# An attention and GLU block on one core: column tiles for the GLU, a finer second chunk, more exponentials on VectorE

## The chip, the cores and the metric

The kernel runs on one core of a Trainium2 chip. The metric is the device time of one execution in microseconds (us). The core has TensorE (PE in the profile; PEld are its weight loads), VectorE (DVE), ScalarE (ACT), GpSimd (POOL) and SyncE (SP), which issues the DMAs. The granted TensorE clock of the profiled execution was 0.998 of full speed.

## The reference, cut to what matters

```python
B, S, D, H, Df = 1, 2048, 640, 32, 1728              # head width 20
x = A_x                                              # bf16, as all weights
n = layernorm(x)
q, k, v = heads(n @ wqkv)                            # (3, H, S, 20)
p = softmax(einsum("bhqd,bhkd->bhqk", q, k) * 20**-0.5)
h = x + merge(einsum("bhqk,bhkd->bhqd", p, v)) @ wo
m = layernorm(h)
out = h + (gelu(m @ w_gate) * (m @ w_up)) @ w_down   # tanh form of gelu
```

The scores are 32 heads of 2048 x 2048 values. Every one of these 134 million values needs an exponential.

## The kernel before, in words

**A planner orders everything.** The kernel does not write instructions in order. Each piece of work is registered with `op` (L58): its engine, a modelled duration, a priority (lower is sooner), what it reads and writes, and the PSUM banks that it takes (`acq`) and gives back (`rel`). `Sched.schedule` (L91) then plays all engines through time and picks, for each engine when it is free, the ready operation of the best priority. The result is a fixed order for each engine's queue, and `emit` (L239) writes it out with semaphore waits. Every instruction goes through one line of `emit`, so L359 of the profile stands for many kinds of work; there the tile names tell them apart. A `Bank` object lists the PSUM banks (0 to 7) that a piece of work may use. The planner knows three array shapes of PE: "row" (weights of 32 rows, four row groups), "col" (weights of at most 32 columns, four column groups) and "full" (128 by 128). For operations of priority 1 and up it prefers the shape that PE is in, since a change has a modelled cost of 0.098 us. When PE would be idle for long it inserts matmuls without use ("warm").

**Chunks, slots and tiles.** The 2048 queries are cut into chunks (`SIZES`, L310): 512, 512, 256, 256, 256, 128, 128. The 32 heads form 8 groups of four heads. A slot is 512 columns of work: one group for a chunk of 512, two groups for 256, four for 128. There are 32 slots in all. Each slot has 64 score tiles of 128 keys by 512 columns: 16 for each of the four heads of a group. A head's 20 values of q and k lie in one of four row groups of 32 rows, so tiles of different heads (index j) can be multiplied at the same time.

**Scores and exponentials.** `unit` (L895) takes two or three tiles in turn: the score matmuls (L919, shape "row") go to PSUM banks 0 to 2 or 3 to 4, and one ScalarE instruction makes the exponentials of all of them (`pts`, or a spare part in `rege`). Some tiles do not go to ScalarE. A quad is the four heads' tiles of one place, and `D_QUADS` (L326) sets how many quads of each slot go to VectorE: none in the first slot, then 3, 3, 3, 2, 2, 2, 1 by chunk, 79 in all. Such a tile ("d tile") is scored behind one of the units, into bank 7 or 5. VectorE scales it into 16-bit integers (L840, four of these for a quad). Then it forms four different terms from all 2048 columns, and each term is multiplied with V; their sum stands in for the exponential. A quad on VectorE so has four PV steps instead of one. Which of the four tiles goes behind which unit is chosen from the quad that comes next, a head not in the unit if there is one.

**PV and the sums.** `pv_op` (L855) multiplies the exponentials with V (21 columns of weights, the last one of ones, so that the row sums come out as well) in shape "col", four heads in four column groups, and adds up in bank 6. `epilogue` (L984) copies a slot's result to `osb`. For all chunks but the last `spread` (L969) sends the sums through DRAM (`sums`, then `rc`), VectorE takes the reciprocals, and they go through DRAM again (`rsums`) to be broadcast into `bsum`. GpSimd multiplies (`on16`), and the result goes to DRAM (`attn`). The last chunk takes a shorter way with PE transposes.

**After a chunk.** `post` (L1040) is registered when the last slot of a chunk is done: load the attention result, out projection (`chain`, L640, 160 matmuls of 320 columns in all), add x, layer norm, transposes, then gate and up (`mms`, L1095: 28 blocks of 128 weights by five steps), gelu, product, and down (L1159, 448 matmuls of 320 columns). These use banks 7 and 5, low priorities, and shape "full". For the first chunk ScalarE computes Gelu itself, which needs another activation table. For later chunks `gelu` (L1028) uses tanh, which lies in the table of the exponentials, and five VectorE instructions around it, with a temporary buffer in the part of `qt_all` that held the second block of 512 queries. The buffers `h_sb`, `hnT` and `ha` hold 512 tokens; a chunk of 256 takes one half (`base`, L963).

**Before the slots** come the layer norm of x and the projections of q, k and v, which run on into the first slots.

Of the kernel before, what the change touches and what calls it, by code (L numbers as in the profile page):

```python
# [16 lines left out]
SEM_ANY = 0.036  # L17
# [4 lines left out]
PE_AGE = 1.5  # L22

# [3 lines left out]
class Bank:  # L27

    __slots__ = ("allowed", "b")

    def __init__(self, *allowed):
        self.allowed = allowed
        self.b = None
# [5 lines left out]
class Op:  # L39
    __slots__ = ("i", "eng", "fns", "dur", "lat", "prio", "deps", "succ", "nd", "ready",  # L40
                 "acq", "rel", "sem", "tag", "mode", "start", "fin", "pos", "know", "util")


class Sched:
# [13 lines left out]
    def op(self, eng, fns, dur, prio, reads=(), writes=(), acq=(), rel=(), after=(), sem=None, lat=None, mode=None, util=0.0):  # L58
        if eng == "dve" and rel and prio > self.ev:
            prio = self.ev  # L60
        o = Op()
        o.i = len(self.ops)
        o.eng, o.dur, o.lat, o.sem = eng, dur, DRAIN[eng] if lat is None else lat, sem
        o.util = util
        o.mode = mode
        o.tag = writes[0] if writes else None
        o.fns = fns if isinstance(fns, list) else [fns]
        o.prio = (prio, o.i)
        deps = set(after)
        for r in reads:  # L70
            if r in self.lw:
                deps.add(self.lw[r])
        for w in writes:
            if w in self.lw:
                deps.add(self.lw[w])
            deps.update(self.rd.get(w, ()))
        for r in reads:
            self.rd.setdefault(r, []).append(o.i)
        for w in writes:
            self.lw[w] = o.i  # L80
            self.rd[w] = []
        deps.discard(o.i)
        o.deps = deps
        o.acq = list(acq)
        o.rel = list(rel)
        o.succ = []
        o.ready = 0.0
        self.ops.append(o)
        return o.i

    def schedule(self):  # L91
# [19 lines left out]
        recent = collections.deque()  # L111
        live = False
        due = None
        total = len(ops)
        while done < total:
# [4 lines left out]
            for e in ENGINES:  # L120
# [8 lines left out]
                while ready[e]:  # L129
# [10 lines left out]
                    for bk in o.acq:  # L140
                        for b in bk.allowed:
                            if owner[b] is None and free_at[b] <= t + 1e-9 and b not in got and b not in kept:
                                got.append(b)
                                break
                        else:
                            got = None
                            break
                    if got is None:

                        if p[0] == 0:  # L150
                            kept.update(bk.allowed[0] for bk in o.acq)
                        skipped.append((p, i))
                        continue
# [20 lines left out]
                if chosen is None:  # L174
                    if e == "pe" and self.warm is not None:
# [4 lines left out]
                        if sum(x for _, x in recent) < WARM_MIN * WARM_WIN and (free7 or live):  # L180
                            o = Op()
                            o.i, o.eng, o.lat = len(ops), "pe", DRAIN["pe"]
                            o.prio, o.sem, o.tag, o.util = (9, 0), None, "warm", 0.213
                            o.acq, o.rel, o.succ, o.dur = [], [], [], 0.215
                            if live and (mode[e] == "col" or not free7):
                                o.fns, o.mode, o.deps = list(self.pad), "col", set()
                            else:
                                b = fb[0]
                                o.fns, o.mode = [self.warm[b]], "full"
                                o.deps = set(self.warm_deps) | ({last[b]} if last[b] is not None else set())  # L190
                                last[b] = o.i
# [6 lines left out]
                if e == "pe" and self.pad is not None and o.tag and o.tag[0] == "O":  # L198
# [10 lines left out]
                o.start = t  # L209
                if e == "act":  # L210
                    due = t + o.dur + (0.905 if o.dur > 1.2 else 1.332) - QK_LEAD if o.mode == "exp" else None
# [9 lines left out]
                for bk in o.rel:  # L221
                    b = bk.b
                    owner[b] = None
                    free_at[b] = o.fin + SEM_LAT.get((e, "pe"), SEM_ANY)
# [85 lines left out]
SIZES = (512, 512, 256, 256, 256, 128, 128)  # L310
# [15 lines left out]
D_QUADS = (3, 3, 3, 2, 2, 2, 1)  # L326
D_QUADS0 = 0
SIX = ()
D_FIRST, D_SPAN = 0, 18
GELU_A = 2.0 * 0.7978845608028654  # L330
# [4 lines left out]
P_QK, P_PV, P_PRO, P_EPI, P_LN, P_BG = 0, 1, 1.5, 2, 2.5, 3  # L335


def bass_sequential_preLN__mha_block__glu_gated_geglu__prompt_kernel(
# [12 lines left out]
    with ExitStack() as es:  # L351
# [42 lines left out]
        rc = sb("rc", [128, 2, 16], FP32)  # L394
        bsum = sb("bsum", [128, 512], FP32)
# [242 lines left out]
        def chain(bk, key, n, steps, reads, prio, acq=True, after=()):  # L638
            for k, (l, r) in enumerate(steps):
                yield op("pe", lambda eng, l=l, r=r, k=k: eng.matmul(  # L640
                    bank(bk, n), l, r, start=(k == 0), stop=(k == len(steps) - 1)),
                    c_mm(n), prio, mode="full", util=n / 2400.0, reads=reads, writes=[key], acq=[bk] if (k == 0 and acq) else [],
                    after=after if k == 0 else ())
# [148 lines left out]
        for s_, (c, gs) in enumerate(slots):  # L792
            mine = list(dict.fromkeys(x[1:3] for x in tiles if x[0] == s_))
            n = D_QUADS[c] if s_ else D_QUADS0
# [5 lines left out]
        while rem:  # L800
# [9 lines left out]
            if k[1] < want:  # L810
                n -= six
                q = d_rem[s_]
                js = [x[3] for x in rem[0:n]]
                near = [x for x in q if x[1:3] == q[0][1:3]]
                xd = min(near, key=lambda x: x[3] in js)
                q.remove(xd)
# [7 lines left out]
        assert not any(d_rem.values())  # L824
        pv_slot, pv_n, pv_ops = [0], [0], []
        pv_start = {}
        pv_wait, d_wait = [], []
        last_qk = {c: [] for c in range(len(CHUNKS))}
# [5 lines left out]
        def d_exp(b, tile, prio):  # L834
            c = slots[tile[0]][0]
            e = min(c, 2)
            h = len(d_raw)
            v, vk = d_v[e][d_n[e] % len(d_v[e])]
            aft = tuple(e_ops) + (tuple(last_qk[0]) if c else ()) + (tuple(last_qk[1]) if c > 1 else ())
# [55 lines left out]
        def unit(u):  # L895
# [39 lines left out]
            qk = op("pe", fns, 0.215, P_QK, mode="row", util=0.0533 * len(al), reads=reads, writes=[("S", u), "qkseq"] + ([("SD", xd)] if six else []), acq=bks)  # L935
            for x in al:
                last_qk[slots[x[0]][0]].append(qk)
            if six:
                bd = bks[2]
            elif xd:  # L940
                bd = Bank(*BG[slots[xd[0]][0]])
                qd = op("pe", [qk_mms(lambda: bank(bd), xd, kk) for kk in range(512 // CHUNKS[slots[xd[0]][0]][1])], 0.08,
                        P_QK + 0.5, mode="row", util=0.0533, reads=qk_reads(xd), writes=[("SD", xd)], acq=[bd], after=[qk])
                last_qk[slots[xd[0]][0]].append(qd)
# [18 lines left out]
        def base(c):  # L963
            n = CHUNKS[c][1]
            if n == 128:
                return 2 + (c == len(CHUNKS) - 1)
            return 2 * (c % 2) if n < 512 else 0

        def spread(s, c, gs, nq):  # L969
            n = len(gs)  # L970
            h = lambda dst, src, reads, key, sem, issue: dma(dst, src, key, reads, sem + str(s), 3.2, P_EPI, issue, keep=False)
            h(sdr[s], osb[DH:128:32, s, :], [("osb", s)], ("sdr", s), "sa", 0.1)
            h(rc[:, s, :], sdr[s].rearrange("j (a b) -> (j a) b", b=16), [("sdr", s)], ("rc", s), "sb", 0.4)
            op("dve", I("reciprocal", rc[:, s, :], rc[:, s, :]), 0.25, P_EPI, reads=[("rc", s)], writes=[("rc", s)])
# [9 lines left out]
        def epilogue(s_, bk):  # L984
# [9 lines left out]
            b2 = Bank(*BG[c])  # L994
# [6 lines left out]
            for tt in range(4):  # L1001
                op("pe", lambda eng, tt=tt: eng.transpose(bank(b2)[:, tt * 128:(tt + 1) * 128],
                                                          osb[:, s, tt * 128:(tt + 1) * 128], identf[:]),
                   c_mm(128, 2.5), P_EPI, mode="full", reads=[("osb", s), "identf"], writes=[key], acq=[b2] if tt == 0 else [],
# [3 lines left out]
            op("dve", lambda eng: eng.reciprocal(rcv, bv()[:, :, :, DH]), 0.17, min(P_EPI, sc.ev), reads=[key], writes=[("rc", s)])  # L1008
            for gi, g in enumerate(gs):
# [4 lines left out]
                   c_dve(80 * nt), min(P_EPI, sc.ev), reads=[key, ("rc", s)], writes=[("on", g, tb + tt) for tt in range(nt)],  # L1014
# [25 lines left out]
        def post(c, banks, tail):  # L1040
            p = P_EPI if tail else P_LN
# [10 lines left out]
            for tt in range(tb, tb + nt):  # L1052
                t = q0 // 128 + tt - tb
                i = t % 2
                if tail:
                    transposes(o_nat[:, 0, :], [("on", g, 0) for g in range(NG)], oT[:, :, tt * 128:(tt + 1) * 128],
                               ("hnT", tt), banks, P_EPI, "act", after=first)
                for hf in range(2):
                    bk = Bank(*banks)
                    key = ("bk", sc_id())  # L1060
                    list(chain(bk, key, 320, [(oT[:, a, tt * 128:(tt + 1) * 128], wo[:, a, hf * 320:(hf + 1) * 320])
                                              for a in range(NA)], [("hnT", tt), "wo"], p, after=(sc.lw[("h", tt, hf)],)))
# [26 lines left out]
            def mms(k, w, wkey, after):  # L1089
                bk, key = Bank(*banks), ("bk", sc_id())  # L1090
                for fi in range(min(fn_, NF - k * fn_)):
                    f = k * fn_ + fi
                    for a in range(NA):
                        st = fi == 0 and a == 0
                        op("pe", lambda eng, a=a, f=f, fi=fi: eng.matmul(  # L1095
                            bank(bk)[:, fi * nq:(fi + 1) * nq], w[:, a, F0[f]:F0[f] + 128], hnT[:, a, 128 * tb:128 * tb + nq],
                            start=(a == 0), stop=(a == NA - 1)),
                           c_mm(nq), p, mode="full", util=nq / 2400.0, reads=hk + [(wkey, 0)], writes=[key], acq=[bk] if st else [],
# [24 lines left out]
            else:  # L1123

                cp, gl = [], []
                for k in range(nb):
# [3 lines left out]
                    if c:  # L1130
# [8 lines left out]
                for ks in [] if c else [list(range(i, min(i + 4, nb))) for i in range(0, nb, 4)]:  # L1139
# [11 lines left out]
            for tt in range(tb, tb + nt):  # L1151
                t = q0 // 128 + tt - tb
                i = t % 2
                for hf in range(2):
                    bk = Bank(*banks)
                    key = ("bk", sc_id())
                    for f in range(NF):
                        o = hb + f * nq + (tt - tb) * 128
                        op("pe", lambda eng, f=f, o=o, hf=hf, bk=bk: eng.matmul(  # L1159
                            bank(bk, 320), ha_f[:, o:o + 128], wd[:, f, hf * 320:(hf + 1) * 320],  # L1160
                            start=(f == 0), stop=(f == NF - 1)), c_mm(320), p, mode="full", util=0.133, reads=hkeys(f // fn_) + [("wd", 0), "wd2", "wdz"],
# [15 lines left out]
                        skip_group_check=True) for b in sc.warm_banks}  # L1177
        sc.pad = [I("matmul", PS[32 * j:32 * j + 32, 512 * 6:512 * 7], zer[:], kt_all[:, 0, 0:512], start=False, stop=False,
                    tile_position=(0, 32 * j), skip_group_check=True) for j in range(4)]
        sc.warm_deps = tuple(sc.lw[kk] for kk in k_keys[0][0])  # L1180
        for kt in range(NT):
            proj_v(kt, 0, (6, 7), P_EPI if kt < 4 else P_BG, "dve")
        
        ui = 0
        for s_, (c, gs) in enumerate(slots):
            if c == 0:
                g = s_
                if g + 1 in STEP:
                    t, (g0, g1) = g + 1, STEP[g + 1]
                    pr = P_EPI if t == 1 else P_BG  # L1190
# [3 lines left out]
                if g < 3:  # L1194
                    for kt in range(NT * g // 3, NT * (g + 1) // 3):
# [60 lines left out]
```

## Time and profile before

| | us |
|---|---|
| median of 3 runs | 899.21 (899.01 to 900.5) |
| the profiled execution | 899.9 |
| its span | 898.2 |
| first exponential starts, last one ends | 35.6, 858.9 |
| busy: PE, ACT, DVE, POOL | 836.4, 851.0, 689.6, 75.0 |
| exponentials on ScalarE: 346 of 1536 columns, mean; 347 of 1024 columns, mean | 1.50, 1.07 |
| d tile evictions on VectorE: 316, mean | 0.687 |
| reciprocals of the sums on VectorE: 30, mean | 0.243 |

How to read it: busy time of PE holds waits, since matmuls are pipelined and their ends are modelled. An instruction's duration overlaps that of the one behind it on its engine, by 0.08 us or so, so that 15 tiles on ScalarE take 6.78 us though the six durations add up to more. In a row of a group, the number behind x is the count, then come busy time and the mean duration, then the idle time of the engine before them.

### The profile page before, as it was taken

How to read it: one execution, taken by the hardware profiler on the slowest of the kernel's cores; microseconds unless marked ns; L12 is line 12 of the kernel's file. 1: busy time of each engine (PE TensorE's matmuls, PEld its weight loads, DVE VectorE, ACT ScalarE, POOL GpSimd, SP SyncE). 2: the span in 40 equal slices, each digit the busy share in tenths (PEclk: the TensorE clock that was granted, in tenths of full speed). 3: DMA queues.
4: the chain of work that ended last, by engine and by line, in shares of the span. 5: the costliest groups of instructions: out<-in, count | busy, mean ns of one | idle time of the engine just before them, and what ended most of it. 6: DMA issues, size and time to landing. Idle time of an engine off the chain costs nothing.

```text
span 898.2 us, 24425 instructions
## 1 busy us (share of the span) xinstructions
PE 836.4 (93%) x10745; PEld 359.1 (40%) x10809; DVE 689.6 (77%) x1263; ACT 851.0 (95%) x777; POOL 75.0 (8%) x147
## 2 busy tenths in 40 slices
PE   3999999899989899999999899999999999999988
PEld 2532222222223222323344333334445446666657
DVE  7839888888989888787778889965669669658553
ACT  6699999999999999999999999999999999999960
POOL 5000000000001100000000100000102000020100
PEclk9999999999999999999999999999999999999999
DMA  7211120222244510000111110011111010031000
GB/s 264 84 50 49 32 67 29 64 81 66 73 137 135 152 46 17 17 14 5 39 51 54 33 34 17 18 30 48 29 54 33 18 48 18 20 63 26 10 17 15
DMA packets 55937, 46.17 MB, mean 51 GB/s; under 512 B 25492, under 2 KB 49392, under 8 KB 55832
## 3 DMA queue, kind: packets, MB, share of 16 engines
q1 hardware_dynamic: 55832, 44.62, 17.8%
q8 instruction: 84, 1.38, 0.6%
q14 instruction: 21, 0.17, 0.1%
HBM read 30.68 MB, written 11.04 MB: 46 GB/s over the span
## 4 chain that ended last, share of the span: by engine, by line
ACT 46%; PE 46%; DVE 6%; issue 1%; DMA 1%; DVEq 0%
ACT pts L359 35%; PE ps L919 14%; PE ps L359 11%; ACT rege L359 10%; PE ps L1095 9%; PE ps L640 6%; PE ps L1159 5%; DVE rege L359 1%; DVE qt_all L359 1%; DVE rege L840 1%; ACT qt_all L359 1%; DVE stats L359 1%; DVE rege L1131 1%; PE ps L585 1%; DMA rege<-xn_t 1%
## 5 line engine op out<-in xcount | busy, mean ns | idle before, releaser
L359 ACT ACTIVATE pts<-ps 128x1536 bf16<-128x1536 f32 x578 | 652.6, 1242 | 10.2 <-PE ps L919 5.7
L919 PE MATMUL ps<-qt_all,kt_all 32*128 32x256 bf16 (+2 forms) x3584 | 320.8, 288 | 25.7 <-ACT pts L359 16.7
L919 PEld LDWEIGHTS ps<-qt_all,kt_all 32*128 32x128 bf16 x3584 | 103.3, 92 | 236.0 <-ACT pts L359 128.3
L840 DVE TENSOR_SCALAR rege<-ps 128x512 int16<-128x512 f32 x200 | 137.0, 687 | 58.6 <-PE ps L919 56.4
L359 ACT ACTIVATE rege<-ps 128x1536 bf16<-128x1536 f32 x115 | 172.1, 1496 | 1.5 <-PE ps L359 0.7
L1095 PE MATMUL ps<-rege,regw 128*128 128x256 bf16 (+2 forms) x951 | 151.6, 289 | 8.4 <-DVE rege L359 2.9
L359 PE MATMUL ps<-pts,v_all 128*21 128x256 bf16 (+2 forms) x2472 | 134.0, 287 | 0.0
L359 PE MATMUL ps<-rege,v_all 128*21 128x512 bf16 (+2 forms) x1564 | 127.6, 312 | 1.3 <-DVE rege L359 1.0
L840 DVE TENSOR_SCALAR qt_all<-ps 128x512 int16<-128x512 f32 x116 | 79.8, 688 | 42.5 <-PE ps L919 40.9
L1095 PEld LDWEIGHTS ps<-rege,regw 128*128 128x128 bf16 x980 | 74.2, 99 | 65.7 <-issue 31.5
L359 POOL TENSOR_TENSOR on<-osb,bsum 128x512 bf16<-128x512 f32 x30 | 42.0, 1399 | 648.2 <-DMA bsum<-rsums 648.1
L359 DVE TENSOR_SCALAR rege<-rege 128x2048 int16<-128x2048 int16 x132 | 92.7, 717 | 2.1 <-PE ps L359 1.2
L640 PE MATMUL ps<-regw 128*128 128x512 bf16 (+1 forms) x340 | 82.0, 349 | 4.6 <-issue 1.7
L1159 PE MATMUL ps<-regw,rege 128*128 128x320 bf16 x448 | 83.7, 302 | 1.1 <-DVE rege L1120 0.5
L359 PEld LDWEIGHTS ps<-pts,v_all 128*21 128x21 bf16 x2472 | 54.3, 91 | 32.4 <-issue 24.4
L359 DVE TENSOR_SCALAR qt_all<-qt_all 128x2048 int16<-128x2048 int16 (+2 forms) x111 | 64.7, 594 | 2.0 <-PE ps L359 1.0
L359 PEld LDWEIGHTS ps<-rege,v_all 128*21 128x21 bf16 x1564 | 41.0, 90 | 45.9 <-issue 23.6
L359 PE MATMUL ps<-qt_all,v_all 128*21 128x256 bf16 (+2 forms) x1048 | 53.7, 282 | 1.7 <-DVE qt_all L359 1.6
L1159 PEld LDWEIGHTS ps<-regw,rege 128*128 128x128 bf16 x448 | 36.6, 97 | 35.8 <-issue 20.1
L359 DVE TENSOR_SCALAR qt_all<-rege 128x2048 int16<-128x2048 int16 x70 | 48.9, 707 | 0.9 <-PE ps L359 0.4
L640 PEld LDWEIGHTS ps<-regw 128*128 128x128 bf16 x360 | 28.9, 98 | 47.5 <-issue 25.0
L1148 DVE TENSOR_TENSOR rege<-rege,ps 128x512 bf16<-128x512 bf16 (+1 forms) x53 | 35.8, 677 | 15.6 <-PE ps L1095 15.4
(98 smaller groups left out, 503.2 us busy)
## 6 DMA issues: line engine op xcount, KB each, us to landing
bsum<-rsums SPq DMA_DIRECT2D x120, 64.0 KB, 2.0
rege<-in_A_x_dram SPq DMA_DIRECT2D x6, 640.0 KB, 5.1
q_rows<-regw SPq DMA_DIRECT2D x20, 128.0 KB, 1.9
out_dram<-rege SPq DMA_DIRECT2D x16, 160.0 KB, 2.2
attn<-on SPq DMA_DIRECT2D x120, 20.0 KB
regw<-in_B_w_gate_dram SPq DMA_DIRECT2D x5, 432.0 KB, 3.3
regw<-in_B_w_up_dram SPq DMA_DIRECT2D x5, 432.0 KB, 3.2
kt_all<-k_rows SPq DMA_DIRECT2D x12, 160.0 KB
```

The source lines that it names most:

```text
L359: return lambda eng: getattr(eng, method)(*args, **kwargs)
L585: op("pe", lambda eng, a=a: eng.transpose(bank16(bk, D)[:, 128 * a:128 * a + 128], src[:, a * 128:(a + 1) * 128], ident[:]), 0.055, prio, ...
L640: yield op("pe", lambda eng, l=l, r=r, k=k: eng.matmul(bank(bk, n), l, r, start=(k == 0), stop=(k == len(steps) - 1)), c_mm(n), prio, mode ...
L840: d_ops.append(op("dve", lambda eng: eng.tensor_scalar(v[:, 512 * h:512 * h + 512], bank(b), EXP_MUL, -32000.0, ALU.mult, ALU.max), c_dve( ...
L919: return lambda eng: eng.matmul(out()[:, kk * nq:(kk + 1) * nq], kt_all[32 * j:32 * j + 32, g, kt * 128:(kt + 1) * 128], qt_all[32 * j:32 ...
L1095: op("pe", lambda eng, a=a, f=f, fi=fi: eng.matmul(bank(bk)[:, fi * nq:(fi + 1) * nq], w[:, a, F0[f]:F0[f] + 128], hnT[:, a, 128 * tb:128 ...
L1131: op("dve", lambda eng, bg=bg, fv=fv, w=w: eng.tensor_scalar(fv, bank(bg, w), 0.5, None, ALU.mult), c_dve(w), p, reads=[kg], writes=hkeys( ...
L1148: hdone.append(op("dve", lambda eng, bu=bu, fv=fv, w=w: eng.tensor_tensor(fv, fv, bank(bu, w), ALU.mult), c_dve(w), p, reads=[ku] + hkeys( ...
L1159: op("pe", lambda eng, f=f, o=o, hf=hf, bk=bk: eng.matmul(bank(bk, 320), ha_f[:, o:o + 128], wd[:, f, hf * 320:(hf + 1) * 320], start=(f = ...
```

## The change: what it does

- **Chunks.** The second chunk of 512 becomes two of 256: 512, five of 256, 128, 128. Still 32 slots.
- **Quads on VectorE.** The count is set by slot: 0, then 27 slots with 3, two with 2, two with 1: 87 in all.
- **Heads matched.** The units that carry a d tile are taken four at a time, and of all ways to hand the four tiles to the four units the one with the fewest repeated heads is kept. The planner also models the row groups: a score operation's time counts from when its row groups and banks are free. A d tile's scores wait up to 0.6 us for PE to be in shape "row".
- **Column tiles.** Each matmul of out projection, gate, up and down with 128 weight columns becomes four with 32 each, at the four column groups, in shape "col". The projections of q, k, v stay "full".
- **Sums.** The reciprocal leaves VectorE: GpSimd makes a first guess by integer arithmetic on the bits and three Newton steps, ten small instructions, each waiting for the one before. The planner's latency for the hops through DRAM goes from 3.2 to 2.6 us.
- **Gelu.** Chunks that start before token 768 use Gelu on ScalarE (so the first half of the old second chunk too), the others tanh.
- **Late banks and the tail.** Once all score operations are placed, the work after a chunk may use banks 0 to 4 as well. The last chunk's own steps get priority 1.2 instead of 2, ahead of VectorE evictions of the chunk before it (1.8).

```diff
-SIZES = (512, 512, 256, 256, 256, 128, 128)
+SIZES = (512, 256, 256, 256, 256, 256, 128, 128)
-D_QUADS = (3, 3, 3, 2, 2, 2, 1)
-D_QUADS0 = 0
+D_SLOT = (0,) + (3,) * 27 + (2,) * 2 + (1,) * 2
+HOP = 2.6
+TANH_FROM = 768
+P_QK, P_PV, P_TAIL, P_PRO, P_EPI, P_LN, P_BG = 0, 1, 1.2, 1.5, 2, 2.5, 3
+LATE = (0, 1, 2, 3, 4)
...
-                        for b in bk.allowed:
+                        for b in bk.allowed if scores else bk.allowed + bk.after:
...
+                    if got and 0 < p[0] < 1 and mode[e] != "row" and t - o.ready < SD_AGE and scores > 1:
+                        skipped.append((p, i))
+                        continue
...
+                if o.rows:
+                    if mode[e] == "row":
+                        b = max([row_start + 0.01] + [freed[x.b] for x in o.acq] + [row_end[j] for j in o.rows])
...
+                    o.dur = max(0.012, b + 0.215 - t)
...
+        def col4(out, l, r, start, stop):
+            return [lambda eng, j=j: eng.matmul(out()[32 * j:32 * j + 32], l[:, 32 * j:32 * j + 32], r, start=start, stop=stop,
+                                                tile_position=(0, 32 * j), skip_group_check=True) for j in range(4)]
...
-                q = d_rem[s_]
-                js = [x[3] for x in rem[0:n]]
-                near = [x for x in q if x[1:3] == q[0][1:3]]
-                xd = min(near, key=lambda x: x[3] in js)
-                q.remove(xd)
+                xd = d_rem[s_].pop(0)
...
+        with_d = [u for u, xd in enumerate(dtile) if xd]
+        for i in range(0, len(with_d), 4):
+            us = with_d[i:i + 4]
+            used = [[x[3] for x in units[u]] for u in us]
+            best = min(itertools.permutations([dtile[u] for u in us]),
+                       key=lambda p: sum(x[3] in js for x, js in zip(p, used)))
+            for u, x in zip(us, best):
+                dtile[u] = x
...
-            op("dve", I("reciprocal", rc[:, s, :], rc[:, s, :]), 0.25, P_EPI, reads=[("rc", s)], writes=[("rc", s)])
+            x, y, z = rc[:, s, :], rn[:, 0, :], rn[:, 1, :]
+            d = lambda fn, r, w: op(POOL, fn, 0.25, P_EPI, reads=r, writes=w)
+            d(I("tensor_scalar", y.bitcast(I32), x.bitcast(I32), -1.0, RECIP_MAGIC, ALU.mult, ALU.add), [("rc", s)], ["ry"])
+            for i in range(3):
+                d(I("tensor_tensor", z, x, y, ALU.mult), [("rc", s), "ry"], ["rz"])
+                d(I("tensor_scalar", z, z, -1.0, 2.0, ALU.mult, ALU.add), ["rz"], ["rz"])
+                d(I("tensor_tensor", x if i == 2 else y, y, z, ALU.mult), ["ry", "rz"], [("rc", s) if i == 2 else "ry"])
...
-            p = P_EPI if tail else P_LN
+            p = P_TAIL if tail else P_LN
...
-                    bk = Bank(*banks)
+                    bk = Bank(*banks, after=LATE)
...
-                    if c:
+                    if q0 >= TANH_FROM:
...
-                        op("pe", lambda eng, f=f, o=o, hf=hf, bk=bk: eng.matmul(
+                        fn = col4(lambda bk=bk: bank(bk, 320), ha_f[:, o:o + 128], wd[:, f, hf * 320:(hf + 1) * 320], f == 0,
+                                  f == NF - 1) if COL else lambda eng, f=f, o=o, hf=hf, bk=bk: eng.matmul(
```

The same replacement by `col4` is made in `chain` for the out projection and in `mms` for gate and up.

## The prediction

> **What bounds the kernel now.** I read the page first, then busy time by stage, then the shapes on ScalarE, then the chain that ended last, then the timeline where a price was missing. From the page (engine totals; ScalarE in 40 slices; the chain by engine):
>
> ```profile
> PE 836.4 (93%) x10745; PEld 359.1 (40%) x10809; DVE 689.6 (77%) x1263; ACT 851.0 (95%) x777; POOL 75.0 (8%) x147
> ACT  6699999999999999999999999999999999999960
> ACT 46%; PE 46%; DVE 6%; issue 1%; DMA 1%; DVEq 0%
> ```
>
> Two engines look full. The stages tell which one counts (length, then busy time of PE, PEld, DVE, ACT, POOL):
>
> ```profile
> 100.00:300.00 200.00, 185.19 (x1597) 53.18 (x1618) 175.24 (x309) 198.62 (x176) 16.56 (x23) 1.00 0.28 80
> 300.00:850.00 550.00, 528.41 (x7904) 240.90 (x7937) 422.38 (x736) 547.15 (x484) 45.09 (x91) 1.00 0.14 35
> ```
>
> ScalarE is busy 99.3% and 99.5%, VectorE 87.6% and 76.8%. PE's 96% holds waiting too: its matmuls are pipelined, and the waits name 128.3 us in which a weight load for scores stood until ScalarE had freed a PSUM bank. So from the first exponential (35.6 us) to the last (ends 858.9 us) the time is the amount of work on ScalarE. Behind it lies a tail of 898.2 - 858.9 = 39.3 us. In the chain that ended last (start, length, what, count):
>
> ```profile
> 51.48 5.43 ACT pts L359 x5
> 58.26 5.44 ACT pts L359 x5
> 849.31 0.33 PE ps L359 x16
> 850.75 0.56 PE ps L359 x32
> 851.64 0.78 PE ps L359 x48
> 867.73 0.98 DVE rege L1131 x2
> 870.13 1.06 ACT qt_all L359
> 875.01 6.36 PE ps L1095 x101
> 881.37 3.81 PE ps L1159 x28
> 885.17 5.71 PE ps L1095 x102
> 891.38 3.99 PE ps L1159 x28
> ```
>
> The first two rows recur every 6.78 us, which is six exponentials, three of three tiles and three of two: 15 tiles, 0.452 us a tile. The three PV rows are matmuls of 128 columns in four column tiles: 16 more cost 0.22 to 0.23 us, 14 ns each, so a step of four takes 55 ns; 102 full matmuls of the same width (885.17) take 56 ns each. The last rows are the tail: 203 gate/up matmuls start after 875, and the last chunk owns only 140. The other 63, and the 28 at 881.37, belong to the chunk before it.
>
> **The change, part by part.**
>
> *87 quads instead of 79.* 32 tiles leave ScalarE: 32 x 0.452 = 14.5 us off the engine that bounds. VectorE gets 8 quads of four evictions (687 ns) and four terms (717 ns): at most 5.6 us each, 45 us, all in the eight slots from about 532 to 746 us, which had two quads each. PE gets 8 x 3 further PV quads of 0.22 us, 5 us, and loses 13 score units.
>
> *Chunk two as two of 256; its first half on Gelu.* Before, all of chunk 512 to 1023 used tanh. Now its first half uses Gelu, which needs the table changed and changed back:
>
> ```profile
> 371.50 1.28 ACT L359 ACT_TABLE_LOAD   x1
> 372.80 6.46 ACT L359 ACTIVATE rege<-rege 128x2048 bf16<-128x2048 bf16 x4
> 379.27 1.28 ACT L359 ACT_TABLE_LOAD   x1
> ```
>
> By the 6.46 us for 7168 columns, 3584 take 3.3 us, beside 2.56 us of loads; the 3.5 tanh of 1024 columns that go took about 1.0 us each. ScalarE: +2.4 us. VectorE loses 3.5 gelu rounds (three products of 746, 729 and 682 ns, two scalings of 448 ns, about 2.7 us after overlap): -9 us. The score and PV matmuls of this chunk halve in width and double in number, the same streaming time. The second effect is order. The windows of gate/up alone (L1095) show no matmul from 425 to 500 and three from 500 to 525, and down (L1159) none from 470 to 600: chunk one has finished, chunk two ends its scores only at 433.8 us, and its out projection, statistics and transposes stand alone. Halves in alternating buffers let one half's GLU run beside the other's preparation.
>
> *Column tiles for out projection, gate/up and down.* 1728 steps of one matmul become four each. By the PV rows the streaming time stays (55 against 56 ns), so I cost the steps at 0, and both ends at 1728 x (-1 to +9 ns; 9 if a 16-matmul burst in 0.28 us were the rule) = -2 to +15 us of PE, of which only the tail's 168 steps (up to 1.5 us) have no cover. What goes is the change of array shape: a quad alone among other shapes (start 147.34, next start 147.67) takes 0.33 us, one after another quad (149.40 to 149.62) 0.22 us, so a change costs 0.105 us. Over the matmuls in order of start I count 1624 changes, 220 of them between full array and column tiles: 23 us of PE work saved, hidden behind ScalarE in the main stage, but it is what the GLU backlog is made of.
>
> By the Trainium skill ("TensorE: Matmul & The Clock Gate", the section on 56 against 53.3 ns) consecutive matmuls start at least about 25 ns apart, which speaks against this change: a step of four would take 100 ns. By it 280 steps of 128 columns cost 44 ns more, some 12 us, and the sum would be about 892; the trace's 14 ns within column bursts disagrees.
>
> *Heads matched to free rows.* Score matmuls in distinct row groups run together (147.03, two of them, 0.39 us; 148.43, four, 0.40 us); with a group taken twice it is 0.60 us (140.57, three). So a mismatch costs 0.21 us of PE, 0 to 316 times, up to 66 us; hidden as long as ScalarE is the bound. I take 0.
>
> *Sums inverted on GpSimd.* 30 reciprocals of 243 ns (7.3 us) leave VectorE, which never stood waiting before them (idle 0.0). Ten GpSimd instructions come instead in each slot. Timeline rows of GpSimd and VectorE:
>
> ```profile
> 84.27 1.27 POOL L359 TENSOR_TENSOR on<-osb,bsum 128x512 bf16<-128x512 f32 x1 [69.71 <-DMA bsum<-rsums]
> 84.42 1.67 DVE L359 TENSOR_SCALAR rege<-rege 128x2048 int16<-128x2048 int16 x1
> 292.35 0.20 POOL L359 TENSOR_TENSOR nw<-nw 128x4 f32<-128x4 f32 x1
> 292.64 0.73 POOL L359 TENSOR_SCALAR nw<-nw 128x4 f32<-128x4 f32 x1
> ```
>
> Small ones start 0.28 us apart, some stretch to 0.73: the chain gets 3 to 5 us longer per slot. Behind it on SP's queue stand the write of the inverted sums, the four broadcasts, the attention writes, and whatever transfer of h or transpose was ordered after; SP waited 119.8 us for these sums already, and their reader is the post work of a chunk many us later. Cover gone, this would cost 3 to 5 us once per chunk. The first two rows show the danger: a VectorE term (0.685 us normally) took 1.67 us beside the large GpSimd product. Bounds for 300 small ones: 0 (no other VectorE instruction beside the small chains was stretched) to 0.28 us each (33 terms that overlapped GpSimd at all had a mean of 965 ns, the others 683), 84 us of VectorE. I take 0, the small chains being the nearest rows. The Trainium skill ("GPSIMD Engine Reference", Specifications) says that the engine shares its SBUF interfaces with VectorE, and names contention with VectorE's two-port modes; the trace agrees with 1.67 us.
>
> *Priorities and late banks.* Once all scores are issued, the GLU may use banks 0 to 4 beside its two; the last chunk's own steps go ahead of the chunk before. In the chain between 862.8 and 873.5 some 4.9 us are the earlier chunk's: evictions 0.55, 0.70, 0.98, gelu steps 0.69, 0.33, 0.60, tanh 1.06. After 875 it owns 63 x 0.056 = 3.5 us and 28 downs, 3.8 us. Together 12.2 of the 39.3 us can go if that chunk is done, or yields. It needs about 14 us of PE sooner; PE gets 23 us from shape changes and the GLU-free stretch around 425 to 525. Between 0 and 12.2 I take 8, nearer the upper end, because PE gets enough but VectorE gets fuller. With no cover for the fuller VectorE I add 1.5 us of ScalarE idle.
>
> VectorE from 300 to the last exponential: 422 + 45 - 9 - 5 (reciprocals) + 10 (evictions moved out of the tail) = 463 of 538 to 550 us, 84 to 86%. The first stage above ran at 87.6% with ScalarE at 99.3%, so this fits.
>
> **Sum.** Against the profiled execution (899.9 us, span 898.2, 1.7 around it): -14.5 + 2.4 + 1.5 - 8 = -18.6, 881.3. That execution lies 0.7 above the median of 899.21, so against the median 880.6; I say 880.5.
>
> **Rivals.**
> 1. *The tail stays.* VectorE's 45 us delay the GLU evictions, and the last chunk but one is again late. For it: the 45 us fall just where PE caught up. Against: 85%. Time: 880.5 + 8 = 888.5, range 886 to 893.
> 2. *PE is the true bound from 300 on.* For: 96% busy. Then the exponentials gain only what PE gains. Against: ScalarE's 99.5%, and PE loses work. About 893 to 897; without effect altogether 899.
> 3. *Slower: GpSimd holds VectorE up.* At 0.28 us for each small instruction the stage from 470 on (39 quads at 5, GLU 120, slot ends 9: 324 of 377 us) takes 45 more, 98%. The fullest windows with ScalarE unharmed are 23.35 and 23.56 of 25 us, 94%; at 94% the 369 us take 393, +16, and the tail's 8 are not won: about 904. It decides from about 0.2 us per instruction (356 us, 94%). Against it: the small chains of before.
> 4. *Column steps dearer than PV's.* If the four matmuls of a step started 25 instead of 14 ns apart, the 280 steps of 128 columns would take 100 instead of 56 ns, 12 us late in the run: about 892. Against it: the PV rows. (The page named above would give this.)
> 5. *Better*: the whole 12.2 us and more of the tail: 868 to 872.
>
> **How the numbers follow.** Forecast (872 to 886) 0.62, better 0.06, rival 1 0.12, rivals 2 and 4 with a gain 0.06; no change 0.04 (within 0.2%, about what a measurement of this kernel can tell: its runs spread over 0.17%); slower 0.10. So faster 0.86, same 0.04, slower 0.10. 869 to 895 leaves out the slower, the unchanged and a rest of 4 in 100.
>
> **What would show it.** Right: 680 exponentials instead of 693; ten table loads; last exponential near 848; no full-array matmul after the projections but transposes and warmers; gate/up spread without a gap at 425 to 525; the 128-column gate/up of the chunk before the last beginning before the last exponential; tail near 31 us. Wrong: ScalarE idle before scores above some 5 us; terms with a mean above 0.8 us; a column step of 128 above 65 ns; VectorE over 94%.

## The result: 0.8% slower, and the profile after

The changed kernel takes 907.5 us (median of 4, 904.09 to 908.4), the kernel before beside it 899.69 us. The ratio is 1.0077, with a 95% interval of 1.006 to 1.0094. Forecast were 880.5 us and a range of 869 to 895. The profiled execution took 904.09 us with a span of 902.4 us, against 899.9 and 898.2 before. It was the quickest of the four, so the profiles below account for 4.2 us, while the medians lie 7.8 us apart.

The page after (totals, code blocks, chain), then busy time by stage (length; PE, PEld, DVE, ACT, POOL):

```profile
PE 848.0 (94%) x17855; PEld 424.2 (47%) x17855; DVE 714.9 (79%) x1283; ACT 836.0 (93%) x763; POOL 168.9 (19%) x461
q8 instruction: 139, 2.28, 1.0%
ACT 50%; PE 43%; DVE 5%; issue 2%; DVEq 0%
```

```profile
100.00:300.00 200.00, 192.48 (x2319) 64.38 (x2315) 174.84 (x302) 199.15 (x177) 40.33 (x106) 1.00 0.31 87
300.00:850.00 550.00, 533.43 (x13246) 294.46 (x13236) 446.79 (x761) 541.89 (x477) 109.25 (x304) 0.99 0.14 34
```

ScalarE is nearly as full as before (98.5% of the long stage, 99.5% before) and its work is 15 us smaller (836.0 against 851.0). VectorE stands at 81% in the long stage. Two things have grown: "issue" in the chain, from 1% to 2%, and the number of packets on queue q8, each a block of code. The page before has 84 of them, against 139:

```profile
q8 instruction: 84, 1.38, 0.6%
```

On ScalarE's timeline the last exponentials, then the table for the tail:

```profile
847.90 2.44 ACT L388 ACTIVATE pts<-ps 128x1536 bf16<-128x1536 f32 x2 [0.70 <-PE ps L958]
850.36 1.28 ACT L388 ACT_TABLE_LOAD   x1
```

So the last exponential ends at 850.3 us, 8.6 earlier than before. The tail is 902.4 - 850.3 = 52.1 us, 12.8 longer. The chain in the tail (start, length, what; "issue" is time in which PE waited for nothing that the profile shows):

```profile
869.49 1.97 PE ps L669 x128
871.46 1.50 issue
872.96 1.97 PE ps L669 x128
874.93 1.77 issue
876.71 1.97 PE ps L669 x128
878.68 1.50 issue
880.18 1.97 PE ps L669 x128
882.15 1.50 issue
```

L669 is the column-tile helper. Each run is exactly 128 matmuls, with their 128 weight loads 256 instructions, and then PE stands still. A block of code is 2.28 MB / 139 = 16.4 KB, and PE's 17855 matmuls and 17855 weight loads make 257 instructions for each of the 139. The runs start 3.47 or 3.75 us apart. So PE has used up a block after 1.97 us and gets the next one 3.47 us after the last (108 ns for a step of four). Within a run the matmuls start 13.8 ns apart (from 872.96 to 874.71), 55 ns a step. I summed the stops over 0.45 us of this kind after 850, each from the start of the last matmul ahead of it to the next start: nine, 12.8 us, just what the tail grew by. (The "issue" rows of the chain, which begin where that matmul ends, add up to 10.7 us.) Steps of 320 columns, 112 matmuls in 4.02 us, need some 4.6 us a block and do not stop.

The Trainium skill ("Runtime: NRT & Kernel Launch", Instruction fetch mechanics) describes code streamed in 16 KiB blocks of 256 instructions. The packet count agrees. It also says that the loading hides behind the pace of issue; the 1.5 us stops here contradict that.

### The profile page after: what moved, and what is told of

Read it like the earlier page. It is cut to its first block, busy times and chain, and to the rows that moved or that the text cites. A ratio compares the mean times of both kernels' runs of the same rounds, so it can differ in the third digit from the quotient of the medians.

```text
span 902.4 us, 38928 instructions
## 1 busy us (share of the span) xinstructions
PE 848.0 (94%) x17855; PEld 424.2 (47%) x17855; DVE 714.9 (79%) x1283; ACT 836.0 (93%) x763; POOL 168.9 (19%) x461
## 3 DMA queue, kind: packets, MB, share of 16 engines
q8 instruction: 139, 2.28, 1.0%
## 4 chain that ended last, share of the span: by engine, by line
ACT 50%; PE 43%; DVE 5%; issue 2%; DVEq 0%
ACT pts L388 37%; PE ps L669 16%; PE ps L958 12%; ACT rege L388 11%; PE ps L388 10%; PE ps L674 3%; DVE qt_all L388 1%; DVE rege L879 1%; DVE rege L388 1%; ACT L388 1%; DVE stats L388 1%; PE ps L615 1%; ACT qt_all L388 1%; DVE qt_all L879 0%; DVE kt_all L388 0%
## 5 line engine op out<-in xcount | busy, mean ns | idle before, releaser
L388 ACT ACTIVATE pts<-ps 128x1024 bf16<-128x1024 f32 (+1 forms) x567 | 641.9, 1264 | 12.5 <-PE ps L958 8.7
L958 PE MATMUL ps<-qt_all,kt_all 32*128 32x256 bf16 (+2 forms) x4096 | 321.1, 273 | 13.8 <-ACT pts L388 7.8
L958 PEld LDWEIGHTS ps<-qt_all,kt_all 32*128 32x128 bf16 x4096 | 114.6, 92 | 216.2 <-ACT pts L388 110.1
L879 DVE TENSOR_SCALAR rege<-ps 128x512 int16<-128x512 f32 x216 | 147.9, 686 | 49.0 <-PE ps L958 46.3
L669 PE MATMUL ps<-rege,regw 128*32 128x256 bf16 (+2 forms) x4480 | 169.6, 274 | 13.1 <-issue 11.0
L388 PE MATMUL ps<-rege,v_all 128*21 128x256 bf16 (+2 forms) x1916 | 131.1, 291 | 2.1 <-DVE rege L388 1.8
L669 PEld LDWEIGHTS ps<-rege,regw 128*32 128x32 bf16 x4480 | 96.2, 96 | 49.4 <-issue 31.3
L879 DVE TENSOR_SCALAR qt_all<-ps 128x512 int16<-128x512 f32 x132 | 90.5, 686 | 33.3 <-PE ps L958 32.4
L669 PE MATMUL ps<-regw,rege 128*32 128x320 bf16 x1792 | 82.0, 302 | 1.9 <-issue 0.5
L388 PE MATMUL ps<-qt_all,v_all 128*21 128x256 bf16 (+1 forms) x1408 | 63.2, 265 | 2.7 <-DVE qt_all L388 2.4
L669 PEld LDWEIGHTS ps<-regw,rege 128*32 128x32 bf16 x1792 | 42.9, 96 | 21.7 <-issue 8.3
```

What stands on the lines that cost most here:

```text
L388: return lambda eng: getattr(eng, method)(*args, **kwargs)
L669: return [lambda eng, j=j: eng.matmul(out()[32 * j:32 * j + 32], l[:, 32 * j:32 * j + 32], r, start=start, stop=stop, tile_position=(0, 32 ...
L879: d_ops.append(op("dve", lambda eng: eng.tensor_scalar(v[:, 512 * h:512 * h + 512], bank(b), EXP_MUL, -32000.0, ALU.mult, ALU.max), c_dve( ...
L958: return lambda eng: eng.matmul(out()[:, kk * nq:(kk + 1) * nq], kt_all[32 * j:32 * j + 32, g, kt * 128:(kt + 1) * 128], qt_all[32 * j:32 ...
```

## Experiments

Four theories were put to the test. **A**: code loading costs the time, since PE uses its blocks of instructions up faster than they come. **B**: column tiles as such are dear. **C**: VectorE's 45 us or GpSimd's small instructions are. **D**: the planned order of PE is late whatever the array shape. All times are medians. "Last exp." and "tail" come from each kernel's profiled execution, and the tail runs from the end of the last exponential to the end of the span. A few us in these two columns need not be the edit: the profiled executions of e3, e5, e12 and e13 lie 5 to 7.5 us above their medians, and after, e2, e5 and e8 have PE's work in the same order up to about 843 us, but for single matmuls, and yet end their exponentials between 847.4 and 857.3 us.

| run | what | us | ratio to before, 95% | last exp. | tail |
|---|---|---|---|---|---|
| before | | 899.7 | 1 | 858.9 | 39.3 |
| after | | 907.5 | 1.0077 (1.006 to 1.0094) | 850.3 | 52.1 |
| e1_full | after, full matmuls | 898.0 | 0.998 (0.996 to 1.000) | 843.8 | 52.1 |
| e2_narrow_full | after, 128-column gate/up full | 888.2 | 0.986 (0.984 to 0.989) | 847.4 | 38.9 |
| e3_before_col | before, column tiles | 915.2 | 1.015 (1.012 to 1.018) | 867.2 | 51.3 |
| e5_two_tiles | after, 128-column gate/up in two tiles | 892.8 | 0.992 (0.990 to 0.995) | 857.3 | 40.4 |
| e6_recip_dve | e2, reciprocals on VectorE | 896.3 | 0.997 (0.995 to 0.999) | 849.4 | 44.2 |
| e7_quads79 | e2, 79 quads | 896.7 | 0.997 (0.996 to 0.998) | 861.3 | 35.4 |
| e8_no_late | e2, no late banks | 894.7 | 0.993 (0.990 to 0.995) | 852.8 | 40.9 |
| e9_one_512 | e2, second chunk of 512 | 900.2 | 1.001 (1.000 to 1.003) | 842.1 | 55.6 |
| e10_old_match | e2, old choice of d tiles | 901.0 | 1.001 (1.000 to 1.003) | 859.0 | 41.8 |
| e11_before_87 | before, 87 quads | 904.7 | 1.005 (1.003 to 1.007) | 843.5 | 59.2 |
| e12_wide_full_late | e2, last 256 chunk's gate/up full | 888.2 | 0.989 (0.984 to 0.993) | 855.5 | 38.3 |
| e13_recip_dve_hop | e6, hop latency 3.2 | 901.6 | 1.003 (1.000 to 1.007) | 865.8 | 41.4 |
| e14_less_dve | e11, less VectorE work | 901.7 | 1.002 (1.001 to 1.003) | 842.9 | 58.4 |
| e15_half_down | e11, less PE work | 881.3 | 0.980 (0.979 to 0.982) | 844.6 | 34.4 |
| e16_91 | e2, 91 quads | 895.0 | 0.995 (0.992 to 0.998) | 842.1 | 52.7 |

### What the column tiles cost

```diff
# e1_full
-COL = True
+COL = False
# e2_narrow_full, in mms (both places)
-if COL
+if COL and nq > 128
# e5_two_tiles, in mms
-fn = col4(...)
+fn = (col4 if nq > 128 else col2)(...)     # col2: two tiles of 64 weight columns
# e3_before_col: before.py, with col4 in chain, mms and down
```

> The changed kernel with out projection, gate/up and down as full 128x128 matmuls again; all else of the change stays. Theory A (PE's instructions arrive in blocks of 256, one every 3.47 us or so, and steps of four column matmuls use them up faster): no stall of PE that ends with 'issue' and lasts over 0.5 us, tail 36 to 41 us instead of 52, time 886 to 895 us. Rival C (VectorE's 45 us more and GpSimd's 300 small instructions cost the time): 900 us or more, tail near 50 us. Rival D (the gain of ScalarE is lost because the planned order of PE is late whatever the shape): tail 45 to 50 us, 897 to 903 us.

> The changed kernel with column tiles kept for steps of 256, 320 and 512 columns, and only gate/up of 128 columns (280 steps) as full matmuls. Theory A: a step of 256 columns needs 8 instructions in 109 ns, just what arrives, one of 128 columns 8 in 55 ns, so only these stall: the 12.8 us of issue gaps after 850 go, and the time is 888 to 894 us. Rival B (column tiles are dear at any width): less than half of the gain of the run with full matmuls everywhere. Rival C: 900 us or more.

> The kernel before with one part of the change alone: out projection, gate/up and down as four column tiles. Theory A: its tail holds 280 steps of 128 columns, 56 ns each now, 108 ns at one block of 256 instructions in 3.47 us: up to 14.6 us more, less what fewer shape changes save: 906 to 914 us, with issue gaps of 1.5 us in the tail. Rival C: 895 to 900 us, since VectorE and GpSimd are as before.

> The changed kernel with gate/up of 128 columns as two column tiles of 64 weight columns instead of four of 32: still column tiles, but 4 instructions a step instead of 8. Theory A: 256 instructions last 64 steps, about 3.6 us at 56 ns, as long as a block needs to arrive: the issue gaps in the tail nearly go, 889 to 896 us. Rival B (tiling as such is slow, for its weight loads or for shape changes): gaps and time stay, 902 to 908 us. Rival C: 902 to 908 us, too.

Taking the 280 narrow steps out of the column tiles gains 19 us over the changed kernel, and the result, 888.2 us, beats both kernels. Its chain in the tail, where L1140 is the full-array gate/up:

```profile
863.16 6.09 PE ps L1140 x109
869.25 3.92 PE ps L669 x112
873.16 5.76 PE ps L1140 x101
878.92 0.02 issue
```

No stop is left in the tail; five remain ahead of it, between 752 and 841 us, 3.6 us together. Theory B falls with e5: it still has column tiles, only with 4 instructions a step instead of 8, and its narrow steps run through in the tail but for one short stop at its start (0.35 us at 858), here 308 matmuls in 8.79 us, 57 ns a step:

```profile
874.30 0.04 issue
874.34 8.79 PE ps L673 x308
887.05 3.27 PE ps L673 x112
```

e5 also keeps the planned order: PE's runs of matmuls of one kind follow each other in its trace just as in the changed kernel's, 2493 in each. So its gain of 14.7 us speaks against theory D as the cause of the loss.

Column tiles alone, on the kernel before, cost 15 us, a little more than expected; the stops are there again (chain of e3):

```profile
900.60 0.94 issue
901.54 1.97 PE ps L640 x128
903.51 1.40 issue
904.91 1.97 PE ps L640 x127
906.88 1.68 issue
```

So A is shown, and C is out as the cause of the 19 us. A part of the 19 us may be the clock: its granted mean was 0.994 to 0.996 in the four executions of the changed kernel and 1.0 in the four of e2. The two profiled ones lie 16.1 us apart, and 13.2 of these are the tail, in which the clock was full in both.

But e1 missed its range of 886 to 895 at 898. Its tail is 52.1 us with no stop in it; the time is in D's range, the tail above it. Full matmuls everywhere bring back the shape changes (1625 in order of start, against 1469 in e2; at the prediction's 0.105 us, 16 us of PE). That PE's work reaches into the tail for this reason is an estimate that no run tests by itself. Wide column tiles are a gain (9.8 us from e1 to e2), narrow ones a loss.

```diff
# e12_wide_full_late
-if COL and nq > 128
+if COL and c < 5
```

> The same version with gate/up of the last chunk of 256 as full matmuls too (their work lies at 740 to 860 us, beside score and PV matmuls of 128 columns, where PE runs 64 to 70 instructions per us and a block of 256 every 3.47 us gives 74). Theory A: the issue gaps of 3 us there go, and the rest depends on what the shape changes cost: 884 to 889 us. Without effect of code loading in the main stage: 890 to 894 us, for the shape changes alone.

The result equals that of e2, at the slow end of A's range. The profiled execution, which lies 7.4 us above the median, still has three stops at 760 to 769 us, 2.7 us together. Nothing follows but that what the fewer instructions win there and what the shape changes lose about cancel.

### Why the 87 quads gained nothing by themselves

```diff
# e11_before_87: before.py
-D_QUADS = (3, 3, 3, 2, 2, 2, 1)
+D_SLOT = (0,) + (3,) * 27 + (2,) * 2 + (1,) * 2
# e7_quads79: e2
-D_SLOT = (0,) + (3,) * 27 + (2,) * 2 + (1,) * 2
+D_SLOT = (0,) + (3,) * 19 + (2,) * 10 + (1,) * 2
```

> The kernel before with one part of the change alone: 87 quads on VectorE, by slot as in the changed kernel. If VectorE has room (prediction): last exponential 14 us earlier, tail as before, 884 to 888 us. If VectorE's 45 us push the GLU into the tail, as the two runs with and without the split suggest: tail 50 us or more, 896 to 902 us.

> The same version with 79 quads on VectorE, by slot as in the kernel before, instead of 87. ScalarE gets 14.5 us back: last exponential 13 to 15 us later than 847.4. Theory E (the tail is as long as before, 38.9 us, because VectorE's 45 us delay the GLU evictions): tail 31 to 34 us, 894 to 898 us. Theory F (the tail is set by PE, whose backlog VectorE does not make): tail 36 to 40 us, 899 to 903 us.

With 87 quads and nothing else the last exponential comes 15.4 us sooner (14.5 was predicted). The tail grows by 19.9 us, and the time lies above both expected ranges. In the version e2 the quads do pay, by 8.6 us: 14 us sooner, and 3.5 us more tail. e7 does not decide between E and F: its time is in E's range, its tail between the two. On the kernel before with 87 quads two runs tell whose time the tail is.

```diff
# e14_less_dve: e11, in gelu
-            op("dve", I("tensor_scalar", z, z, GELU_B, GELU_A, ALU.mult, ALU.add), ts, p, reads=[zk], writes=[zk])
-            op("dve", I("tensor_tensor", z, z, fv, ALU.mult), tt, p, reads=hk + [zk], writes=[zk])
...
-            op("dve", I("tensor_scalar", z, z, 1.0, None, ALU.add), ts, p, reads=[zk], writes=[zk])
# e15_half_down: e11, in post
-                    for f in range(NF):
+                    for f in range(0, NF, 2):
```

> The kernel before with 87 quads (904.65 us, tail 59.2 us), with three of the five VectorE instructions of each gelu round left out (the polynomial's scaling and second product, and the added one), so that another function than gelu is computed: about 1.6 us less on VectorE in each of some 21 rounds, 33 us in all, PE unchanged. Theory E (VectorE's time sets the pace of the GLU): the tail falls by 8 us or more, 890 to 897 us. Theory F (PE's time sets it): 900 to 904 us, tail 55 us or more.

> The kernel before with 87 quads, with every second step of the down projection left out, so that only half of the hidden values reach the output: 224 matmuls of 0.137 us, 31 us less on PE, VectorE unchanged. The last two chunks' own steps give 4 us of that in any case. Theory F (PE's time sets the pace): the tail falls by 12 us or more, 888 to 893 us. Theory E: by 4 to 6 us, 898 to 901 us.

Stage from 300 to 843 us of e11, e14 and e15 in turn (the columns as above):

```profile
300.00:843.00 543.00, 528.69 (x8146) 233.40 (x8143) 442.91 (x758) 538.03 (x474) 43.06 (x77) 1.00 0.14 34
```

```profile
300.00:843.00 543.00, 518.04 (x8112) 234.25 (x8157) 425.02 (x716) 539.99 (x476) 42.35 (x77) 1.00 0.14 35
```

```profile
300.00:843.00 543.00, 512.05 (x8071) 231.28 (x8124) 454.92 (x793) 538.88 (x477) 48.05 (x91) 1.00 0.14 35
```

VectorE has 26 us less to do in e14, 18 of them in this stage, and the tail stays at 58.4 us. In e15 31 us less on PE (224 matmuls) take 24.8 us off it, with VectorE fuller than in e11; the time, 881.3, is even below F's range. So it is PE's time. I read it thus: in the kernel before, PE's work after 300 us just fits into the time that the exponentials take. Ending them 15 us sooner moves 15 us of PE work behind them, and the quads' own PV steps (24 of 0.22 us, 5 us) come on top, 20 us against the 19.9 measured. Whose time the tail of e2 is was not tried in this way. The tail of e11 holds 628 matmuls, that of before 396:

```profile
860.71 15.85 PE ps L1094 x217
876.56 7.61 PE ps L1158 x56
884.17 4.63 PE ps L1094 x83
```

(Chain of e11: gate/up, then down of the last chunk of 256 and the steps of two small chunks, all after 860.)

```diff
# e16_91: e2
-D_SLOT = (0,) + (3,) * 27 + (2,) * 2 + (1,) * 2
+D_SLOT = (0,) + (3,) * 29 + (2,) * 2
```

> The version with full matmuls for gate/up of 128 columns (888.15 us) with 91 quads instead of 87 (three in each slot up to the last two, which have two): 7.2 us less on ScalarE, 22 us more on VectorE, 3 us more on PE. If the gain of each quad is paid back as in the kernel before (there 8 quads gained 15 us and lost 20), 888 to 895 us; if there is room left, 882 to 887 us.

In the profiled execution four more quads end the exponentials another 5.2 us sooner and lengthen the tail by 13.8: paid back, and more. It had PE's clock at half for 6.8 us; the two of the six executions with a granted clock of 1.0 took 890.7 and 891.7 us, about 3 us more than e2.

### The other parts

```diff
# e9_one_512: e2
-SIZES = (512, 256, 256, 256, 256, 256, 128, 128)
+SIZES = (512, 512, 256, 256, 256, 128, 128)
-TANH_FROM = 768
+TANH_FROM = 512
# e8_no_late: e2 (the second value stands in a longer line)
-LATE = (0, 1, 2, 3, 4)
+LATE = ()
-P_TAIL = 1.2
+P_TAIL = 2
# e10_old_match: e2, with the lines of before.py that choose xd from near, and without the permutations
# e6_recip_dve: e2, with the one reciprocal of before.py in spread; e13_recip_dve_hop: e6 with
-HOP = 2.6
+HOP = 3.2
```

> The same version with the second chunk as one of 512 again, on tanh. The prediction gave the split 2.4 us more on ScalarE (two table loads and Gelu for tanh), 9 us less on VectorE, and no gap in the GLU. If the gap was what the backlog of PE is made of, undoing the split makes the tail 5 us or more longer: 892 to 900 us. If not, the table loads alone count: 885 to 889 us.

> The same version without the late banks (0 to 4 for the work after the last scores) and with the last chunk's steps at priority 2 again. The prediction gave the shorter tail, 8 us, partly to these: if that holds, the tail grows by 4 us or more, 892 to 900 us. If the tail is bare PE work, as 38.9 us suggests: 887 to 891 us.

> The version with full matmuls for gate/up of 128 columns (888.15 us), with the old choice of which d tile goes behind which unit. The prediction costed the matching at nothing, since 0.21 us of PE for each mismatch hide behind ScalarE: then 886 to 891 us. If PE's backlog makes the tail, some 40 mismatches come back as 8 us of PE work, the tail grows by 3 us or more: 892 to 898 us.

> The version with full matmuls for gate/up of 128 columns (888.15 us), and the sums inverted on VectorE again, one reciprocal of 0.24 us per slot in place of ten GpSimd instructions. Theory A (code loading explains the loss, GpSimd is harmless): 886 to 891 us. Rival C (the small GpSimd instructions hold VectorE up by 0.2 us or more each): at least 5 us faster, 883 or less, terms on VectorE shorter than 717 ns in the mean.

> The version with the sums inverted on VectorE (896.31 us) and the planner's latency for the hops through DRAM at 3.2 us again instead of 2.6. If the 8 us of that run came from VectorE standing in wait for sums that land later than planned (3.3 us in its trace): 889 to 893 us. If they came from the reciprocals' own 7.3 us on VectorE: 894 to 898 us.

The split is worth 12 us, just above the range, and its place is where the prediction had it: without it the exponentials end 5.3 us sooner and the tail is 55.6 us. The gap in the GLU is back in e9's trace: no gate, up or down matmul starts from 455.9 to 517.2 us, while e2 has no such pause over 12 us between 300 and 850. That the gap is PE time lost for good is argued; e9 also brings back tanh and its VectorE work, which no run separates.

The matching of heads is worth 13 us where nothing was predicted and at most 10 expected. In e10's profiled execution 11.6 us of loss lie before the last exponential, but PE's clock was at half there for 10.2 us in two stretches, so how much of it is the edit is open. The quickest of its ten executions, 897.8 us, is 8 us above the slowest of e2.

The reciprocals on GpSimd are worth 8 us, and e6 missed both of its ranges. The terms on VectorE take 717 ns in the mean with GpSimd doing them and without, so GpSimd holds VectorE up no more than before. The longer hop latency does not explain the 8 us: e13 is slower still and outside both ranges (898.3 to 916.7 us in ten executions; the median without the slowest is 900.4). Why 7 us of VectorE work cost 8 us when 26 us in e14 gave 3 is open.

The late banks look worth 6.6 us, but only 2 us of it lie in the tail, where 4 or more were expected. The rest lies in a stretch where PE's order in e8 and e2 is the same but for some twenty single matmuls, and e8's execution had PE's clock at half for 6.8 us there. Its three executions with a granted clock of 1.0 took 891.0, 892.3 and 894.7 us; how much is the edit is open.

## Why the prediction was wrong, point by point

- **Column tiles, "I cost the steps at 0 ... the tail's 168 steps (up to 1.5 us) have no cover".** This step failed. The streaming time was right, 55 ns a step within a block. The cost is the number of instructions: 8 per step, one block of 256 per 3.47 us, so 108 ns a step. The PV rows that I took as proof were bursts of up to 48 matmuls, shorter than a block. A sustained run could not be read from them. Rival 4 had nearly the right price (12 us; the stops in the tail were 12.8 us) with the wrong cause, and was given a few chances in a hundred. No rival named code loading.
- **87 quads, "VectorE gets ... 45 us" and fits.** The 14.5 us on ScalarE came as worked out, and VectorE had room. What failed is the conclusion that the time before the tail is ScalarE's work alone and the tail a thing of its own. Rival 2, PE as the true bound from 300 us on, comes nearest to what e11, e14 and e15 show on the kernel before; it got 0.06 together with rival 4. ScalarE's 99.5% did not speak against it, since PE was full as well; both ended together.
- **The tail, "between 0 and 12.2 I take 8".** Without the stops (e2) it is 38.9 us, so 0.4 came. The sum of PE work gained was set against the backlog without the 12 us that the exponentials end sooner. The sum itself was too large: counted in the same way, the shape changes fall from 1624 to 1465, by 159 and not 220, since changes between full array and the scores' row shape (782, then 204) became changes between column and row shape. At 0.105 us that is 17 us, not 23.
- **Heads matched, "I take 0"; reciprocals, "I take 0".** They are worth 13 and 8 us by the medians of e10 and e6. Both zeros rest on the cover by ScalarE. That it was not there, since PE was full as well, fits the 13 us but is not shown for either.
- **Gelu and the split.** Two extra table loads came (507.9 and 512.5 us, 1.28 each, Gelu 3.29 us between), as worked out. There are eight loads in all, not ten, because the tail has two fewer. The gap in the GLU was read rightly.
- **The last exponential** was predicted at 858.9 - 14.5 + 2.4 + 1.5 = 848.3; it came at 850.3 in the changed kernel and 847.4 in e2. Rival 3 (GpSimd holds VectorE up) is out: the terms' mean stayed at 712 ns, before and after.

In sum, of the predicted -18.6 us the -10.6 before the tail came as -8.6, and the tail came out at +12.8 instead of -8. The median of the changed kernel lies another 3.4 us above this execution, which no profile explains.

## What to carry to other kernels

An engine's instructions have a price of their own: before replacing one instruction by four, count instructions per us over the longest run without pause, not over a burst, and compare with the spacing of code blocks in the trace. When two engines are both full, taking work from one can show up as a longer tail on the other; test this by leaving out work on each in turn. Here the wide column tiles, which save shape changes, were worth keeping and the narrow ones were not, and undoing that alone turned 0.8% slower into 1.4% faster.

## What the runs showed of the hardware that I had not expected

PE got no block of 256 instructions sooner than 3.23 us after the one before, in any of these profiles; the packets themselves took 1.1 us in the mean. What the rest of the time goes into is not shown. And PE's clock falls to half in the middle of a run in which PE counts as nearly busy throughout. Windows of the changed kernel, then of e2 (the eighth figure, after POOL, is the granted clock):

```profile
625.00:650.00 25.00, 24.23 (x488) 12.06 (x488) 22.02 (x39) 23.76 (x22) 4.38 (x12) 0.89 0.07 18
650.00:675.00 25.00, 24.72 (x543) 12.91 (x535) 17.43 (x28) 23.68 (x21) 3.92 (x11) 0.97 0.16 46
```

```profile
625.00:650.00 25.00, 23.83 (x530) 12.62 (x526) 23.58 (x41) 24.67 (x23) 4.90 (x12) 1.00 0.07 18
650.00:675.00 25.00, 24.52 (x535) 12.43 (x531) 18.40 (x31) 24.88 (x22) 3.20 (x10) 1.00 0.20 54
```

The clock was at half for 6.8 us from 644.4, and ScalarE lost 2.1 us against e2 in these 50 us. In e10 such a stretch at 316 us stands beside a wait of 4.4 us on ScalarE. The profiled executions of e5, e8, e12, e13 and e16 have stretches of 6.8 us too, all near 277 to 318 or near 645 us; the others have none of that length. What sets it off was not tried.
